# A new hand-written order for the start of an attention-plus-MLP kernel, with ten instead of twelve head pairs turned by TensorE and a changed end

## The chip, the cores and the metric

The kernel runs on one core of one Trainium2 chip. The metric is the device time of one execution in microseconds (us); the number quoted for a kernel is the median of several executions. One execution is also profiled; all rows shown below are from such an execution.

## The reference, cut to what matters

Eight batches of twelve heads, 448 tokens, 64 numbers per head. Soft-capped attention, and then a two-layer network over the 3584 tokens, whose activation is a maximum of two products:

```python
scores = scale * q @ k.T                    # per head, 448 x 448
scores = cap * tanh(scores / cap)           # cap = 30
attn = exp(scores - max); attn /= sum
x = (attn @ v)  ->  [3584, 768]
h1 = x @ w1; h2 = x @ w2                    # 768 -> 1024
out = maximum(h1, h2) @ w_out               # 1024 -> 768
```

## The kernel before, in words

**Algebra.** The maximum of h1 and h2 is written as relu(x @ (w1 - w2)) + x @ w2. So the kernel forms `wd_sb` = w1 - w2 (six blocks of 128 rows, one per 128 columns of x) and `wm_sb` = w2 @ w_out once, at the start, and then computes out = relu(x @ wd) @ w_out + x @ wm.

**Attention.** Two heads are a pair (48 pairs, numbered i), two pairs a quad (24 quads, numbered t). q and k have to lie with the head's 64 numbers along the partitions. For pairs below `NX` TensorE turns them (28 transposes of 64x64 per pair, with `ident` as the moving operand) and VectorE copies them to `qkT`; for later quads a transposing DMA on SP's queue does it. Tokens are taken seven per row (448 = 64 x 7), so six of a row's tokens make three full blocks of 128 keys and the seventh of both heads makes a "left" block.

**The order is written by hand.** `ORDER` is a text of steps, run through a table `STEPS`; each step issues its instructions to fixed engines, and every engine runs its own instructions strictly in the order in which the text put them. The place of a load in the text therefore only says what it stands behind on POOL's queue. The steps that are spoken of:

- On POOL's queue: `lk i`, `lq i` (load k or q of a pair, cast to bf16 by the DMA; for pairs from NX on, k is loaded in two parts and all runs are 64 numbers long), `lv t p` (v of a quad in four parts: two for `vp`, two for `vl`), `lw1 c`, `lw2 c` (a 128-row block of w1, w2), `lwo h` (half of w_out), and `sub c 1` (the subtraction that makes block c of `wd_sb`). `sub c 0` is the same on VectorE.
- On PE: `X i` (turn a pair), `W c` (turn a block of w2), `P c h n` (n of the eight matmuls, 128x384, that make a block of `wm_sb`), `S i j` (scores of one key block for the two heads of a pair), `L t` (scores of the left block of a quad), `Y t` (row sums), `V t u` (attn @ v), `M x y n` (n steps of two MLP groups at once, x on the upper and y on the lower 64 rows of the array; -1 is nobody).
- On ACT: `T i j`, `TL t` (tanh of one score tile), `E`, `EL` (exp). On DVE: `XC`, `WC`, `PC` (copies of what PE turned or premultiplied out of PSUM), `Y1` to `Y3` and `N` (normalize into `xT`), `A`, `B` (sums of exps), `ev g` (evacuate group g).
- On SP: `cr t` (the transposing DMA of a quad), `st b t` (store 128 rows of the result).

There are 120 MLP groups; `stage1` groups have 6 blocks of 128 rows and `stage2` groups 14. A group's 128-row block is done as two half matmuls of 64 rows, and two groups share the array, one on each half. Group 0 needs all six blocks of `wd_sb`. The last two groups, 118 and 119, are the two halves (384 columns each) of the last 128 rows of the result.

**Buffers that tie queues together.** `kqs` has two buffers, one for even and one for odd quads; a load of q or k for quad t waits until quad t-2 was turned. `vp`/`vl` have two buffers; a load of v for quad t waits for `V` of quad t-2. Score tiles have two PSUM buffers, shared by `S`, `L` and `V`. `qkT` has two buffers. The loads from POOL take eight semaphores in turn, so a load is issued only when the load eight places before it has landed.

Of the kernel before, what the change touches and what calls it, by code (L numbers as in the profile page):

```python
# [10 lines left out]
ld0 k; ld0 q; ms; lk 1 0; lq 1 0; lk 2 0; lw2 1; lwo 0; lq 2 0; cd k; lw2 0; cd q; X 0 0; lw2 2; lwo 1; lk 3 0;  # L11
X 1 1; XC 0; lq 3 0; lw1 0; XC 1; S 0 0; S 0 1; T 0 0; W 1 2; T 0 1; S 0 2; WC 1; L 0; T 0 2; lv 0 0; OP 1 0 3;
P 1 0 2; E 0 0 3; S 1 0; lv 0 1; X 2 0; P 1 0 1; XC 2; P 1 0 1; lv 0 2; W 0 1; P 1 0 2; WC 0; TL 0; P 1 0 2;
lv 0 3; W 2 2; PC 1 0; T 1 0; OP 0 0 0; P 0 0 1; WC 2; S 1 1; P 0 0 1; EL 0; P 0 0 1; S 1 2; P 0 0 2; T 1 1;
P 0 0 3; OP 2 0 1; P 2 0 2; PC 0 0; T 1 2; P 2 0 1; S 2 0; P 2 0 2; E 1 0 2; P 2 0 1; S 2 1; P 2 0 2; lw2 3;
OP 1 1 3; P 1 1 2; PC 2 0; P 1 1 2; lq 4 0; T 2 0; P 1 1 4; lq 5 0; E 1 2 3; X 3 2; PC 1 1; T 2 1; S 2 2; XC 3;
lk 4 0; OP 0 1 0; P 0 1 4; T 2 2; sub 0 1; P 0 1 4; OP 2 1 1; P 2 1 1; PC 0 1; L 1; Y 0 3; TL 1; lq 6 0; V 0 0;
Y1 0; E 2 0 3; lw2 4; V 0 1; Y2 0; lk 5 0; Y3 0; S 3 0; lq 7 0; N 0 0; W 3 2; lw1 3; P 2 1 1; N 0 1; T 3 0;
X 4 0; lw2 5; WC 3; lv 1 0; EL 1; S 3 1; XC 4; S 3 2; P 2 1 1; lv 1 1; P 2 1 1; T 3 1; P 2 1 1; W 4 3; lv 1 2;
P 2 1 1; T 3 2; lv 1 3; WC 4; X 5 2; lq 8 0; E 3 0 2; S 4 0; XC 5; S 4 1; lk 6 0; P 2 1 2; OP 4 1 0; P 4 1 1;  # L20
lk 7 0; sub 3 0; P 4 1 4; T 4 0; P 4 1 3; PC 2 1; OP 3 1 3; P 3 1 1; lq 9 0; E 3 2 3; W 5 2; PC 4 1; S 4 2;
WC 5; lw1 2; P 3 1 1; T 4 1; P 3 1 4; T 4 2; lk 8 0; P 3 1 2; OP 3 0 1; P 3 0 1; PC 3 1; lk 9 0; L 2; Y 1 0;
TL 2; lv 2 0; V 1 0; lv 2 1; Y1 1; E 4 0 3; lv 2 2; V 1 1; Y2 1; Y3 1; lv 2 3; S 5 0; lw1 1; N 1 0; X 6 2;
lv 3 0; N 1 1; T 5 0; X 7 3; sub 2 1; XC 6; EL 2; S 5 1; XC 7; S 5 2; X 8 0; T 5 1; X 9 2; XC 8; lv 3 1; T 5 2;
S 6 0; lv 3 2; XC 9; P 3 0 1; E 5 0 2; P 3 0 1; lv 3 3; S 6 1; P 3 0 1; lq 10 0; P 3 0 2; sub 1 0; P 3 0 2;
lk 10 0; OP 5 0 3; P 5 0 1; T 6 0; P 5 0 2; lk 11 0; P 5 0 2; PC 3 0; P 5 0 1; E 5 2 3; P 5 0 1; lq 11 0;
S 6 2; P 5 0 1; lw1 4; OP 4 0 0; P 4 0 1; T 6 1; P 4 0 1; PC 5 0; P 4 0 1; lw1 5; P 4 0 3; T 6 2; P 4 0 1;
lk 12 0; P 4 0 1; L 3; PC 4 0; lk 12 1; Y 2 2; TL 3; lq 12 0; V 2 0; Y1 2; E 6 0 3; lk 13 0; V 2 1; lk 13 1;
Y2 2; Y3 2; lq 13 0; S 7 0; N 2 0; X 10 1; sub 4 1; N 2 1; T 7 0; X 11 3; EL 3; S 7 1; S 7 2; OP 5 1 0;
P 5 1 1; A 3 0 1; P 5 1 1; T 7 1; P 5 1 2; XC 10; sub 5 1; P 5 1 3; T 7 2; P 5 1 1; XC 11; S 8 0; O 0 2;  # L30
M 0 -1 1; PC 5 1; M 0 -1 1; E 7 0 2; M 0 -1 1; S 8 1; M 0 -1 2; A 3 0 2; lv 4 0; M 0 -1 1; O 1 1; M 1 -1 2;
H 0; lv 4 1; M 1 -1 1; T 8 0; M 1 0 1; A 3 1 1; M 1 0 1; lv 4 2; M 1 0 1; O 2 3; M 2 0 1; B 3 0; E 7 2 3;
M 2 0 1; lv 4 3; S 8 2; M 2 0 1; H 1; B 3 1; M 2 1 1; lk 14 0; M 2 1 1; T 8 1; M 2 1 1; ev 0; O 3 0; M 3 1 1;
lk 14 1; M 3 1 2; T 8 2; H 2; A 3 1 2; M 3 2 1; lq 14 0; M 3 2 2; ev 1; O 4 2; M 4 2 1; lk 15 0; L 4; M 4 2 1;
lk 15 1; TL 4; Y 3 1; V 3 0; lq 15 0; Y1 3; E 8 0 3; V 3 1; Y2 3; Y3 3; S 9 0; M 4 2 1; lv 5 0; N 3 0; M 4 3 2;
N 3 1; M 4 3 1; lv 5 1; O 5 1; M 5 3 2; T 9 0; H 4; M 5 3 1; lv 5 2; ev 2; S 9 1; M 5 4 1; ev 3; lv 5 3;
M 5 4 1; EL 4; M 5 4 1; S 9 2; A 4 0 1; O 6 3; M 6 4 3; T 9 1; H 5; A 4 0 2; M 6 5 1; cr 6; M 6 5 2; ev 4;
O 7 0; M 7 5 1; T 9 2; M 7 5 1; S 10 0; H 6; M 7 5 1; M 7 6 1; E 9 0 2; M 7 6 1; ev 5; S 10 1; M 7 6 1; O 8 2;
M 8 6 2; H 7; M 8 6 1; M 8 7 2; ev 6; T 10 0; M 8 7 1; O 9 1; M 9 7 1; A 4 1 1; M 9 7 2; E 9 2 3; lk 16 0; H 8;
S 10 2; ev 7; M 9 8 3; lk 16 1; B 4 0; M 9 8 1; T 10 1; M 9 8 2; lq 16 0; B 4 1; M 9 8 2; T 10 2; M 9 8 2;  # L40
lk 17 0; A 4 1 2; M 9 8 1; O 10 3; M 10 8 2; lk 17 1; M 10 8 1; L 5; lq 17 0; Y 4 0; TL 5; V 4 0; Y1 4; V 4 1;
E 10 0 3; Y2 4; Y3 4; S 11 0; M 10 9 1; lv 6 0; N 4 0; M 10 9 2; M 8 9 1; N 4 1; lv 6 1; M 8 9 3; H 10;
M 8 9 1; lv 6 2; S 11 1; T 11 0; A 5 0 1; M 8 9 2; lv 6 3; M 8 9 1; O 11 0; M 11 9 1; A 5 0 2; EL 5; M 11 9 1;
S 11 2; M 11 9 1; ev 8; M 11 10 2; T 11 1; M 11 10 1; ev 9; M 11 10 1; cr 7; M 11 10 3; T 11 2; M 11 10 1;
S 12 0; M 11 10 1; st 0 0; M 11 10 2; E 11 0 2; O 12 2; M 12 10 1; S 12 1; H 11; M 12 10 2; M 12 11 2; H 10 2;
M 12 11 1; M 10 11 2; H 12; M 10 11 1; T 12 0; A 5 1 1; M 10 11 4; B 5 0; M 10 11 1; E 11 2 3; lk 18 0; O 13 1;
M 13 11 1; S 12 2; M 13 11 1; B 5 1; lk 18 1; M 13 11 1; M 13 12 1; T 12 1; M 13 12 1; ev 10; M 13 12 1;
lq 18 0; M 13 12 2; A 5 1 2; T 12 2; M 13 12 1; lk 19 0; M 13 12 2; ev 11; M 13 12 1; lk 19 1; L 6; Y 5 3;
TL 6; V 5 0; lq 19 0; Y1 5; st 0 1; V 5 1; E 12 0 3; Y2 5; Y3 5; S 13 0; M 13 12 1; lv 7 0; N 5 0; M 13 12 1;
O 14 0; M 14 12 2; H 13; lv 7 1; N 5 1; M 14 12 1; M 14 13 2; lv 7 2; H 12 2; S 13 1; T 13 0; A 6 0 1;  # L50
M 14 13 1; M 12 13 1; lv 7 3; M 12 13 2; H 14; A 6 0 2; EL 6; M 12 13 1; S 13 2; M 12 13 3; T 13 1; M 12 13 1;
O 15 3; M 15 13 1; cr 8; M 15 13 1; ev 12; M 15 13 1; M 15 14 1; T 13 2; M 15 14 1; ev 13; S 14 0; M 15 14 1;
O 16 2; M 16 14 1; E 13 0 2; M 16 14 1; H 15; S 14 1; M 16 14 1; st 0 2; M 16 15 2; ev 14; M 16 15 1; O 17 1;
M 17 15 2; H 16; T 14 0; M 17 15 1; A 6 1 1; M 17 16 3; ev 15; O 18 0; M 18 16 1; E 13 2 3; lk 20 0; S 14 2;
M 18 16 1; H 17; B 6 0; M 18 16 1; lk 20 1; M 18 17 1; T 14 1; M 18 17 1; ev 16; M 18 17 1; lq 20 0; O 19 3;
M 19 17 2; B 6 1; T 14 2; M 19 17 1; lk 21 0; H 18; ev 17; M 19 18 1; lk 21 1; M 19 18 2; A 6 1 2; O 20 2;
M 20 18 1; lq 21 0; M 20 18 2; L 7; ev 18; Y 6 1; TL 7; V 6 0; Y1 6; V 6 1; E 14 0 3; Y2 6; Y3 6; S 15 0;
M 20 19 1; lv 8 0; N 6 0; M 20 19 2; N 6 1; O 21 0; M 21 19 1; lv 8 1; M 21 19 2; H 20; lv 8 2; S 15 1; T 15 0;
# [12 lines left out]
M 28 27 2; H 26 2; A 8 1 2; M 28 27 1; lq 24 0; M 26 27 2; T 18 2; M 26 27 1; lk 25 0; M 26 27 1; L 9; lk 25 1;
Y 8 0; TL 9; V 8 0; Y1 8; lq 25 0; V 8 1; E 18 0 3; Y2 8; Y3 8; S 19 0; M 26 27 1; lv 10 0; N 8 0; M 26 27 3;
# [131 lines left out]
def kernel(  # L204
# [11 lines left out]
    nc = tc.nc  # L216
# [19 lines left out]
    NS = 3
    W2T = 4
    R7 = S // 64
# [178 lines left out]
    def turned_by_pe(t):  # L417
        return 2 * t < NX

# [267 lines left out]
```

## Time and profile before

| | us |
|---|---|
| median of 3 runs (lowest, highest) | 348.4 (348.33, 350.44) |
| the profiled execution | 348.68 |
| its span from first to last instruction | 346.9 |
| PE busy | 327.1 |
| ACT busy | 274.2 |
| DVE busy | 229.5 |
| POOL busy | 175.6 |
| mean granted TensorE clock | 0.99 |

The span is what the profile shows of the profiled execution; 1.78 us of its time lie outside it. Busy time is the union of an engine's instructions. Rows of the timeline give start, duration, engine, line of the code, what was written and read, and in square brackets how long the engine was idle before and what ended that.

### The profile page before, as it was taken

The page shows a single profiled execution, that of the slowest core. Times are in us where ns is not written, and L with a number is a line of the kernel's source. Part 1 is how long each engine was busy: PE and PEld are TensorE (multiplying, and loading weights), DVE is VectorE, ACT ScalarE, POOL GpSimd, SP SyncE. Part 2 cuts the span into 40 slices and gives each one's busy share as a digit, 9 for nine tenths or more (in the row PEclk, how much of TensorE's full clock was granted, in tenths as well). Part 3 has the DMA queues.
Part 4 walks back from the last instruction along what each step waited for, and adds up shares of the span by engine and source line. Part 5 has one row for each costly group of instructions (what it writes and reads, how often), then busy time and mean ns, then how long its engine had stood idle before and what let it go on. Part 6 is the DMA issues. An engine that isn't in the chain of part 4 may idle for free.

```text
span 346.9 us, 9713 instructions
## 1 busy us (share of the span) xinstructions
PE 327.1 (94%) x4100; PEld 197.6 (57%) x4100; DVE 229.5 (66%) x408; ACT 274.2 (79%) x265; POOL 175.6 (51%) x250
## 2 busy tenths in 40 slices
PE   3699997899999999999999999999999999999994
PEld 2355553355586656456656555555875555568762
DVE  3146767488678856886697668768876868774321
ACT  2768999299998999899989998999899989920000
POOL 8338798928437457195592859285658302000000
PEclk9999999699999999999999999999999999999999
DMA  8998999989999999999999999999999964031033
GB/s 128 202 225 158 206 187 192 81 112 86 149 155 112 147 174 107 162 135 99 164 199 118 101 194 215 119 104 170 174 133 109 166 124 79 1 92 49 2 93 91
DMA packets 130988, 46.09 MB, mean 133 GB/s; under 512 B 108288, under 2 KB 125952, under 8 KB 130944
## 3 DMA queue, kind: packets, MB, share of 16 engines
q0 software_dynamic: 93184, 25.74, 74.2%
q1 hardware_dynamic: 37616, 19.50, 28.6%
q8 instruction: 32, 0.52, 0.7%
q10 hardware_dynamic: 144, 0.23, 0.3%
q14 instruction: 12, 0.10, 0.1%
HBM read 48.76 MB, written 11.01 MB: 172 GB/s over the span
## 4 chain that ended last, share of the span: by engine, by line
PE 70%; DMA 12%; ACT 6%; issue 4%; POOL 4%; DVE 4%; SPq 0%; POOLq 0%; DVEq 0%
PE mm L563 52%; PE s L448 7%; PE s L531 5%; DMA osb<-in_moe_w_dram 4%; DMA gT<-in_moe_w_dram 4%; ACT e L469 4%; DMA xT<-in_moe_w_dram 3%; PE s L461 2%; PE s L535 2%; POOL kqs L306 2%; PE mm L506 2%; ACT e L453 1%; POOL wd_sb L356 1%; DVE osb L616 1%; DMA out_dram<-osb 1%
## 5 line engine op out<-in xcount | busy, mean ns | idle before, releaser
L453 ACT ACTIVATE e<-s 128x896 bf16<-128x896 f32 x144 | 127.8, 929 | 14.5 <-PE s L448 10.3
L469 ACT ACTIVATE e<-e 128x2688 bf16<-128x2688 bf16 (+2 forms) x72 | 122.9, 1709 | 0.0
L563 PE MATMUL mm<-wo_sb,gT 64*128 64x384 bf16 x896 | 120.3, 323 | 0.0
L563 PE MATMUL mm<-wm_sb,xT 64*128 64x384 bf16 x672 | 105.6, 323 | 0.0
L563 PE MATMUL mm<-xT,wd_sb 64*128 64x448 bf16 x768 | 101.5, 356 | 4.2 <-POOL wd_sb L356 3.2
L313 POOL DMA_DIRECT2D kqs<-in_k_dram x72 | 53.1, 741 | 77.3 <-DMA qkT<-kqs 77.3
L563 PEld LDWEIGHTS <-gT 64*128 64x128 bf16 x896 | 62.5, 94 | 25.4 <-issue 0.4
L563 PEld LDWEIGHTS <-wd_sb 64*128 64x128 bf16 x768 | 55.6, 95 | 26.0 <-issue 4.6
L563 PEld LDWEIGHTS <-xT 64*128 64x128 bf16 x672 | 52.9, 94 | 19.1 <-issue 1.0
L448 PE MATMUL s<-qkT 64*128 64x448 bf16 x288 | 56.9, 361 | 1.7 <-ACT e L453 1.5
L584 DVE TENSOR_SCALAR gT<-mm 128x448 bf16<-128x448 f32 x64 | 39.7, 621 | 14.5 <-PE mm L563 13.1
L616 DVE COPY osb<-mm 128x384 f32<-128x384 f32 x56 | 30.7, 555 | 27.5 <-PE mm L563 23.7
L481 DVE TENSOR_TENSOR esum<-e 128x896 bf16<-128x896 bf16 x42 | 26.1, 621 | 26.8 <-ACT e L469 15.1
L327 POOL DMA_DIRECT2D vp<-in_v_dram x48 | 30.4, 640 | 21.4 <-PE s L535 17.6
L531 PE MATMUL s<-e,vp 128*32 128x448 bf16 x576 | 35.8, 352 | 0.0
L313 POOL DMA_DIRECT2D kqs<-in_q_dram x36 | 34.8, 967 | 1.2 <-issue 1.1
L465 ACT ACTIVATE el<-s 128x896 bf16<-128x896 f32 x24 | 22.0, 916 | 16.2 <-PE s L461 15.8
L448 PEld LDWEIGHTS <-qkT 64*128 64x128 bf16 x288 | 17.6, 94 | 26.7 <-issue 15.3
L327 POOL DMA_DIRECT2D vl<-in_v_dram x48 | 29.3, 620 | 2.4 <-DMA gT<-in_moe_w_dram 2.4
L544 DVE TENSOR_TENSOR xT<-s,inv 128x448 bf16<-128x448 f32 x48 | 27.7, 620 | 2.6
L481 DVE TENSOR_TENSOR esum<-esum,e 128x896 bf16<-128x896 bf16 x42 | 27.5, 655 | 2.1 <-PE mm L563 0.4
L486 DVE TENSOR_TENSOR esum<-esum,el 64x896 bf16<-64x896 bf16 x42 | 25.9, 617 | 1.8 <-PE mm L563 1.0
(47 smaller groups left out, 235.2 us busy)
## 6 DMA issues: line engine op xcount, KB each, us to landing
out_dram<-osb SPq DMA_DIRECT2D x54, 192.0 KB, 4.2
vp<-in_v_dram POOLq DMA_DIRECT2D x48, 160.0 KB, 6.0
kqs<-in_q_dram POOLq DMA_DIRECT2D x47, 112.0 KB, 4.7
kqs<-in_k_dram POOLq DMA_DIRECT2D x72, 56.0 KB, 3.5
osb<-in_moe_w_dram POOLq DMA_DIRECT2D x4, 512.0 KB, 6.1
gT<-in_moe_w_dram POOLq DMA_DIRECT2D x6, 256.0 KB, 6.8
wo_sb<-in_moe_w_out_dram POOLq DMA_DIRECT2D x2, 768.0 KB, 12.4
kqs<-in_k_dram POOLq DMA_DIRECT2D x11, 112.0 KB, 4.7
```

What stands on the lines that cost most here:

```text
L313: nc.gpsimd.dma_start(out=to, in_=x)
L327: nc.gpsimd.dma_start(out=to, in_=x)
L448: nc.tensor.matmul(s[:, h, :S], k_of(t, o, h, j), q_of(t, o, h))
L453: nc.scalar.activation(expo[i][:, 2 * j : 2 * j + 2, :], slots[i, j][:, :, :S], AF.Tanh, scale=scale / cap)
L469: nc.scalar.activation(e, e, AF.Exp, scale=float(cap))
L481: nc.vector.tensor_add(d, e[:, 0:2, :] if j == 1 else d, e[:, 2 * j : 2 * j + 2, :])
L486: nc.vector.tensor_add(d, d, left_e[t][r, :, :])
L531: nc.tensor.matmul(ps[r, u, :S], vp[t % VB][:, m, 2 * j, u::2], expo[2 * t + o][:, 2 * j + h, :], start=(j == 0), stop=False)
L544: nc.vector.tensor_mul(x, vals[t][:, u, :S], sums[t, 3])
L563: ins = nc.tensor.matmul(self.ps, w[r], x[r], start=first, stop=self.at == [self.n, self.n]).ins
L584: nc.vector.tensor_relu(gT[b // 2][:, f, cs], ps)
L616: nc.vector.tensor_copy(o[:, hs], ps)
```

## The change

- `NX` goes from 12 to 10: pairs 10 and 11 (quad 5) are turned by the transposing DMA (`cr 5`), not by PE.
- For the five quads that PE turns, v is loaded with three tokens per row (two loads of 64 rows x 4 heads x 192 numbers instead of x 320 numbers); `transposes` places k's tokens to match, and `values` picks its block accordingly.
- `transposes` goes through the two 64x64 corners of the array in turn, not seven transposes in one and then seven in the other.
- `ORDER` is new up to the first steps of group 0. `S 0` no longer waits for other work of PE; the last block of w1 (`lw1 4`) stands on POOL's queue behind `lq 10`; four of the six subtractions are VectorE's instead of two. From `L 4` to group 116 the list of PE steps is the same, except for the PSUM banks; the list of ACT's steps is the same throughout, but for the copy at the very end. In POOL's list later on, v of a quad often stands between the k and q of two pairs instead of behind them.
- Groups 118 and 119 are done with whole 128-row matmuls, one after the other (`step(2)`).
- A store of 128 rows is one DMA instead of two. The last group is evacuated in two parts of 192 columns, by VectorE and ScalarE, and each part is stored from a queue of its own (SP, ACT).

The order, first up to group 0 and then at the end:

```diff
-ld0 k; ld0 q; ms; lk 1 0; lq 1 0; lk 2 0; lw2 1; lwo 0; lq 2 0; cd k; lw2 0; cd q; X 0 0; lw2 2; lwo 1; lk 3 0;
-X 1 1; XC 0; lq 3 0; lw1 0; XC 1; S 0 0; S 0 1; T 0 0; W 1 2; T 0 1; S 0 2; WC 1; L 0; T 0 2; lv 0 0; OP 1 0 3;
-P 1 0 2; E 0 0 3; S 1 0; lv 0 1; X 2 0; P 1 0 1; XC 2; P 1 0 1; lv 0 2; W 0 1; P 1 0 2; WC 0; TL 0; P 1 0 2;
-lv 0 3; W 2 2; PC 1 0; T 1 0; OP 0 0 0; P 0 0 1; WC 2; S 1 1; P 0 0 1; EL 0; P 0 0 1; S 1 2; P 0 0 2; T 1 1;
-P 0 0 3; OP 2 0 1; P 2 0 2; PC 0 0; T 1 2; P 2 0 1; S 2 0; P 2 0 2; E 1 0 2; P 2 0 1; S 2 1; P 2 0 2; lw2 3;
-OP 1 1 3; P 1 1 2; PC 2 0; P 1 1 2; lq 4 0; T 2 0; P 1 1 4; lq 5 0; E 1 2 3; X 3 2; PC 1 1; T 2 1; S 2 2; XC 3;
-lk 4 0; OP 0 1 0; P 0 1 4; T 2 2; sub 0 1; P 0 1 4; OP 2 1 1; P 2 1 1; PC 0 1; L 1; Y 0 3; TL 1; lq 6 0; V 0 0;
-Y1 0; E 2 0 3; lw2 4; V 0 1; Y2 0; lk 5 0; Y3 0; S 3 0; lq 7 0; N 0 0; W 3 2; lw1 3; P 2 1 1; N 0 1; T 3 0;
-X 4 0; lw2 5; WC 3; lv 1 0; EL 1; S 3 1; XC 4; S 3 2; P 2 1 1; lv 1 1; P 2 1 1; T 3 1; P 2 1 1; W 4 3; lv 1 2;
-P 2 1 1; T 3 2; lv 1 3; WC 4; X 5 2; lq 8 0; E 3 0 2; S 4 0; XC 5; S 4 1; lk 6 0; P 2 1 2; OP 4 1 0; P 4 1 1;
-lk 7 0; sub 3 0; P 4 1 4; T 4 0; P 4 1 3; PC 2 1; OP 3 1 3; P 3 1 1; lq 9 0; E 3 2 3; W 5 2; PC 4 1; S 4 2;
-WC 5; lw1 2; P 3 1 1; T 4 1; P 3 1 4; T 4 2; lk 8 0; P 3 1 2; OP 3 0 1; P 3 0 1; PC 3 1; lk 9 0; L 2; Y 1 0;
-TL 2; lv 2 0; V 1 0; lv 2 1; Y1 1; E 4 0 3; lv 2 2; V 1 1; Y2 1; Y3 1; lv 2 3; S 5 0; lw1 1; N 1 0; X 6 2;
-lv 3 0; N 1 1; T 5 0; X 7 3; sub 2 1; XC 6; EL 2; S 5 1; XC 7; S 5 2; X 8 0; T 5 1; X 9 2; XC 8; lv 3 1; T 5 2;
-S 6 0; lv 3 2; XC 9; P 3 0 1; E 5 0 2; P 3 0 1; lv 3 3; S 6 1; P 3 0 1; lq 10 0; P 3 0 2; sub 1 0; P 3 0 2;
-lk 10 0; OP 5 0 3; P 5 0 1; T 6 0; P 5 0 2; lk 11 0; P 5 0 2; PC 3 0; P 5 0 1; E 5 2 3; P 5 0 1; lq 11 0;
-S 6 2; P 5 0 1; lw1 4; OP 4 0 0; P 4 0 1; T 6 1; P 4 0 1; PC 5 0; P 4 0 1; lw1 5; P 4 0 3; T 6 2; P 4 0 1;
-lk 12 0; P 4 0 1; L 3; PC 4 0; lk 12 1; Y 2 2; TL 3; lq 12 0; V 2 0; Y1 2; E 6 0 3; lk 13 0; V 2 1; lk 13 1;
-Y2 2; Y3 2; lq 13 0; S 7 0; N 2 0; X 10 1; sub 4 1; N 2 1; T 7 0; X 11 3; EL 3; S 7 1; S 7 2; OP 5 1 0;
-P 5 1 1; A 3 0 1; P 5 1 1; T 7 1; P 5 1 2; XC 10; sub 5 1; P 5 1 3; T 7 2; P 5 1 1; XC 11; S 8 0; O 0 2;
-M 0 -1 1; PC 5 1; M 0 -1 1; E 7 0 2; M 0 -1 1; S 8 1; M 0 -1 2; A 3 0 2; lv 4 0; M 0 -1 1; O 1 1; M 1 -1 2;
...
+ld0 k; ld0 q; ms; lk 1 0; lwo 0; lk 2 0; lq 1 0; lw2 0; cd k; lk 3 0; cd q; lw2 2; X 0 0; lq 2 0; lq 3 0; XC 0;
+S 0 0; S 0 1; T 0 0; T 0 1; S 0 2; T 0 2; lw2 1; E 0 0 3; lwo 1; lk 4 0; X 1 1; XC 1; lv 0 0; W 0 2; lv 0 1;
+L 0; WC 0; S 1 0; TL 0; lv 0 2; OP 0 0 3; P 0 0 1; W 2 0; T 1 0; lv 0 3; EL 0; S 1 1; lw2 3; WC 2; S 1 2;
+X 2 1; T 1 1; X 3 2; XC 2; T 1 2; lv 1 0; W 1 0; XC 3; E 1 0 2; S 2 0; WC 1; S 2 1; P 0 0 7; T 2 0; OP 2 0 1;
+P 2 0 2; PC 0 0; P 2 0 3; E 1 2 3; P 2 0 1; S 2 2; P 2 0 2; T 2 1; PC 2 0; T 2 2; lv 1 1; OP 0 1 2; P 0 1 5;
+lv 1 2; P 0 1 3; OP 2 1 0; P 2 1 1; lv 1 3; P 2 1 1; PC 0 1; P 2 1 3; lw2 5; L 1; Y 0 3; TL 1; lq 4 0; V 0 0;
+lw2 4; Y1 0; E 2 0 3; V 0 1; Y2 0; lq 5 0; Y3 0; S 3 0; lk 5 0; N 0 0; W 3 1; P 2 1 1; N 0 1; lv 2 0; P 2 1 1;
+T 3 0; P 2 1 1; OP 1 0 2; P 1 0 1; WC 3; P 1 0 1; lv 2 1; S 3 1; EL 1; P 1 0 1; PC 2 1; lv 2 2; S 3 2; P 1 0 1;
+T 3 1; P 1 0 2; lv 2 3; P 1 0 2; OP 1 1 3; P 1 1 1; T 3 2; P 1 1 1; PC 1 0; P 1 1 1; lk 6 0; X 4 1; E 3 0 2;
+P 1 1 1; XC 4; P 1 1 4; lk 7 0; S 4 0; PC 1 1; S 4 1; T 4 0; W 4 0; lw1 5; W 5 2; WC 4; E 3 2 3; OP 3 0 1;
+P 3 0 1; lq 6 0; S 4 2; WC 5; X 5 3; T 4 1; lq 7 0; P 3 0 1; XC 5; P 3 0 1; lw1 2; P 3 0 1; T 4 2; P 3 0 2;
+lw1 0; L 2; Y 1 0; TL 2; lq 8 0; V 1 0; lq 9 0; Y1 1; E 4 0 3; V 1 1; lw1 3; Y2 1; Y3 1; S 5 0; N 1 0; P 3 0 1;
+lk 8 0; P 3 0 1; OP 4 1 2; P 4 1 1; N 1 1; P 4 1 2; T 5 0; P 4 1 1; lw1 1; PC 3 0; X 6 3; EL 2; sub 5 0;
+lk 9 0; S 5 1; S 5 2; X 7 0; T 5 1; XC 6; P 4 1 2; T 5 2; XC 7; P 4 1 1; lq 10 0; S 6 0; sub 2 0; P 4 1 1;
+OP 5 0 1; P 5 0 1; E 5 0 2; P 5 0 1; S 6 1; P 5 0 2; PC 4 1; P 5 0 1; lw1 4; P 5 0 3; T 6 0; sub 0 1; OP 4 0 3;
+P 4 0 2; PC 5 0; P 4 0 3; E 5 2 3; P 4 0 1; S 6 2; P 4 0 2; T 6 1; OP 3 1 0; P 3 1 2; PC 4 0; P 3 1 1; lv 3 0;
+P 3 1 2; T 6 2; P 3 1 2; sub 3 0; lv 3 1; L 3; Y 2 2; lv 3 2; TL 3; V 2 0; lv 3 3; Y1 2; E 6 0 3; V 2 1; Y2 2;
+lk 10 0; Y3 2; S 7 0; N 2 0; sub 1 1; X 8 1; N 2 1; X 9 3; T 7 0; XC 8; P 3 1 1; EL 3; S 7 1; XC 9; S 7 2;
+OP 5 1 2; P 5 1 1; lk 10 1; P 5 1 1; PC 3 1; P 5 1 1; T 7 1; P 5 1 1; A 3 0 1; P 5 1 2; lk 11 0; P 5 1 2;
+T 7 2; sub 4 0; O 0 1; M 0 -1 1; lk 11 1; S 8 0; M 0 -1 1; E 7 0 2; M 0 -1 1; S 8 1; PC 5 1; lq 11 0; M 0 -1 3;
...
-M 117 116 7; st 7 4; M 117 116 2; O 118 1; M 118 116 2; H 117; M 118 116 1; M 118 117 2; H 116 2; M 118 117 1;
-M 116 117 2; H 118; M 116 117 6; O 119 3; M 119 117 2; ev 116; M 119 117 1; M 119 118 2; ev 117; M 119 118 7;
-st 7 5; M 119 118 2; M -1 118 2; H 119; M -1 118 1; M -1 119 2; H 118 2; M -1 119 1; M 118 119 8; M -1 119 2;
-ev 118; M -1 119 1; ev 119; st 7 6;
+M 117 115 1; M 117 116 2; ev 115; M 117 116 7; st 7 4; M 117 116 2; M -1 116 2; H 117; M -1 116 1; M -1 117 2;
+H 116 2; M -1 117 1; M 116 117 8; M -1 117 2; ev 116; M -1 117 1; O 118 3; M 118 118 1; ev 117; M 118 118 7;
+st 7 5; M 118 118 6; O 119 0; M 119 119 2; ev 118; M 119 119 12; ev 119; st 7 6;
```

The functions:

```diff
-    NX = 12
+    NX = 10
...
     # load_v
         if part < 2:
             to = vp[t % VB].rearrange("p h j d -> p h (j d)")[r]
-            x = src[:, :, D * a : D * (a + 5)]
+            if turned_by_pe(t):
+                to = to[:, :, : NJ * D]
+                x = src[:, :, NJ * D * a : NJ * D * (a + 1)]
+            else:
+                x = src[:, :, D * a : D * (a + 5)]
...
     # transposes
-            for a in range(2):
-                r = slice(64 * a, 64 * a + 64)
-                for j in range(R7):
-                    to = c * S + j * D
+            for j in range(R7):
+                for a in range(2):
+                    r = slice(64 * a, 64 * a + 64)
+                    to = c * S + (j if c or j == R7 - 1 else 2 * (j % NJ) + j // NJ) * D
                     nc.tensor.transpose(ps[r, to : to + 64], x[r, c * S + j * D : c * S + (j + 1) * D], ident[r, r])
...
     # values
-                    ps[r, u, :S], vp[t % VB][:, m, 2 * j, u::2], expo[2 * t + o][:, 2 * j + h, :], start=(j == 0), stop=False
+                    ps[r, u, :S], vp[t % VB][:, m, j if turned_by_pe(t) else 2 * j, u::2], expo[2 * t + o][:, 2 * j + h, :], start=(j == 0), stop=False
...
     # Group.step
+            if h == 2:
+                w, x = self.unit(self.at[0])
+                self.at = [self.at[0] + 1] * 2
+                nc.tensor.matmul(self.ps, w, x, start=first, stop=self.at[0] == self.n)
+                return
...
     # store
-        for a in range(2):
-            nc.sync.dma_start(out=rows(b, j0 + a, 1)[0], in_=osb[64 * a : 64 * a + 64, :])
+        nc.sync.dma_start(out=rows(b, j0, 2), in_=osb)
...
     # stage2, done
-            nc.vector.tensor_copy(o[:, hs], ps)
-            if b == B - 1 and t == 6:
-                for a in range(2):
-                    to = out[b * S : (b + 1) * S, hs].rearrange("(r j) n -> j r n", j=R7)[R7 - 2 + a]
-                    nc.sync.dma_start(out=to, in_=o[64 * a : 64 * a + 64, hs])
+            if (b, t) != (B - 1, 6):
+                nc.vector.tensor_copy(o[:, hs], ps)
+                return
+            to = out[b * S : (b + 1) * S, :].rearrange("(r j) n -> j r n", j=R7)[R7 - 2 :]
+            mid = half * (DM // 2) + DM // (4 if half else 2)
+            c = slice(hs.start, mid)
+            nc.vector.tensor_copy(o[:, c], ps[:, : mid - hs.start])
+            nc.sync.dma_start(out=to[:, :, c], in_=o[:, c])
+            if half:
+                c = slice(mid, hs.stop)
+                nc.scalar.copy(o[:, c], ps[:, mid - hs.start :])
+                nc.scalar.dma_start(out=to[:, :, c], in_=o[:, c])
...
     # moe
         for _ in range(n):
+            if x == y:
+                groups[x].step(2)
+                continue
```

## The prediction

> **What bounds the kernel now.** I read the page first, for the engines' shares; then windows by stage; then PE's timeline, for a milestone that both kernels pass; then the chain of waits and POOL's timeline for the start; last the end.
>
> ```profile
> PE 327.1 (94%) x4100; PEld 197.6 (57%) x4100; DVE 229.5 (66%) x408; ACT 274.2 (79%) x265; POOL 175.6 (51%) x250
> ...
> 55.00:60.00 5.00, 3.72 (x23) 1.50 (x21) 4.11 (x5) 5.00 (x6) 3.27 (x3) 1.00 1.62 190
> 60.00:65.00 5.00, 3.03 (x16) 1.29 (x18) 1.33 (x3) 1.79 (x3) 5.00 (x6) 0.51 0.52 60
> 65.00:70.00 5.00, 5.00 (x52) 2.41 (x52) 2.83 (x5) 2.03 (x3) 4.17 (x6) 0.81 1.32 93
> ...
> 250.00:300.00 50.00, 49.57 (x635) 29.50 (x626) 37.71 (x68) 47.75 (x46) 18.06 (x27) 1.00 0.88 111
> 300.00:320.00 20.00, 19.07 (x233) 13.70 (x231) 12.43 (x22) 5.99 (x7) 0.00 (x0) 1.00 0.25 61
> 320.00:330.00 10.00, 10.00 (x121) 7.28 (x119) 3.62 (x6) 0.00 (x0) 0.00 (x0) 1.00 0.01 3
> ```
>
> The numbers behind the window's length are busy us of PE, weight loads, DVE, ACT, POOL, then the granted clock, the DMA share and GB/s. ACT is nearly as full as PE while attention lasts, but it ends near 306, and PE then works alone for 36 us. So PE's work and PE's idle time set the end, and time lost early is not regained. The one bad stretch is 55 to 70: PE idles, and the clock falls to 0.51 and 0.81.
>
> The milestone is `L t`, PE's left scores of a quad:
>
> ```profile
> 11.12 0.59 PE L461 MATMUL s<-qkT 64*64 64x448 bf16 x4
> 27.57 0.38 PE L461 MATMUL s<-qkT 64*64 64x448 bf16 x4
> 39.56 0.38 PE L461 MATMUL s<-qkT 64*64 64x448 bf16 x4
> 50.81 0.38 PE L461 MATMUL s<-qkT 64*64 64x448 bf16 x4
> 68.45 0.38 PE L461 MATMUL s<-qkT 64*64 64x448 bf16 x4
> 80.41 0.38 PE L461 MATMUL s<-qkT 64*64 64x448 bf16 x4
> ```
>
> L0 to L5. Two intervals stand out: L0 to L1 takes 16.45 us and L3 to L4 17.64, where the others take 11.25 to 12.0. The chain of waits and POOL's rows tell why:
>
> ```profile
> 3.19 6.43 DMA gT<-in_moe_w_dram
> 9.91 14.55 DMA osb<-in_moe_w_dram
> 50.58 9.15 DMA xT<-in_moe_w_dram
> 59.79 2.13 POOL wd_sb L356
> 61.97 2.79 PE mm L563 x12
> ```
>
> The last block of w1 is issued at 50.58 and lands at 59.73; POOL subtracts until 61.9; group 0 waits for it (idle 0.80 and 2.44 us).
>
> **The change, part by part.** From L4 to group 116 the steps of PE and ACT are the same list, so this stretch keeps its length: cost 0. What hides the rest there: a v load now stands ahead of the second pair's q and k in POOL's queue; these then land some 11 us after `L t`, and their transposing DMA is due 1.5 periods (18 us) after it. If that cover went, PE would wait at `S` by what is over, every period. The merged stores take 27 issues of about 0.6 us off SP, which waits anyway: 0. So the working is for L4, and for the end.
>
> Prices of PE work, start to start in dense stretches at full clock: P 0.174 (12 in 2.09, 46.86 to 48.95); S 0.29; X 0.62 a pair (56 transposes in 1.23, 42.56 to 43.79); L 0.31; Y with both V 2.28 (39.88 to 42.16); W 0.5; a slot of M 0.187 at 448 columns.
>
> (a) *Up to L1.* `T 0 0` needs one turned pair, not two: 0.45 us earlier, 7.3. `S 0 2` no longer stands behind `W 1`, so ACT's wait of 1.74 goes and exp of pair 0 ends at 12.2. But `X 1` needs `lq 1`, now behind the first half of w_out. Landings before: 5.7 for the first load; w_out's half takes 4.1 behind its predecessor (3.71+10.0 against 9.62); a q or k 0.6; and the first big load takes 1.4 more than later ones of its size. So X1 at 5.7+4.2+1.4+1.2 = 12.5. At the slow early speed (56 transposes 2.26, a W 0.95) X1, W0 (its block lands at 13.75) and L0 give L0 at 14.7, 3.6 *later* than before. Then the second pair has what it needs: `lq 2`, `lq 3`, `lw2 1` land by 18, where before PE stood 2.07 for w_out and ACT 3.0. ACT's list from 14.7 gives `T 2 0` near 21; PE is at `S 2 1` near 20.4. From there to L1 are 28 P and one S: 4.87+0.29, so L1 = 25.7, against 27.57: **-1.9**. Bounds: without the 1.4 X1 starts at 11.1 and the gain is 3.3; with the slow clock lasting to 24 it is 0.
>
> (b) *L1 to L2.* 25 P instead of 24: +0.17. (c) *L2 to L3.* 33 P for 23, +1.74; two X for four, -1.25; ACT was without idle here, so half the relief elsewhere counts: **+0.4** for b and c, before the transposes.
>
> (d) *L3 to L4.* Work before: L 0.31, Y and V 2.28, six S 1.74, two X 1.25, eight P 1.39, 25 M slots 4.7: 11.65; it took 17.64. So the waits of 3.24 cost 5.99 with the slow clock behind them. After: one P more, 11.8; L1 to L2 took 12.0 for 11.3 of such work, so 12.2 to 12.4. Does w1 come in time? `lw1 4` stands behind `lq 10`, which waits for `X 7`. By the prices X7 ends 5.9 before L3; `lq 10` issues in 0.97, so `lw1 4` goes out 4.9 before L3. Group 0 asks for block 4 at its fifth step, 7.2 after L3; the DVE subtraction takes 1.23. So 10.8 us for a load that took 6.9 and 9.15 at the same place before: just enough. `sub 1 1`, POOL's later one, ends 3 after L3, and is asked for at 6.3. **-5.3**.
>
> (e) *Transposes in turn.* No row has two 64x64 corners alternating. Upper bound: full overlap, as the two halves of M have (0.163 a pair of 384 columns): 0.31 a pair saved. Lower: 0. The nearest row is `L`, whose four matmuls go through all four corners and take 0.31 for 4x0.187: overlap by two. I take a third of the bound over the six pairs between L1 and L4: **-0.6**; ACT's pace, 11.25 a quad, takes the rest.
>
> The Trainium skill ("TensorE: Matmul & The Clock Gate", Part 1, "Wait — 56ns, not 53.3ns?") says that matmuls start no less than about 25 ns apart however small; the rows here have 1.23/56 = 22 ns, slightly below. By the page (e) would be 0 and the sum 0.6 higher.
>
> (f) *The end.*
>
> ```profile
> 341.28 1.20 DVE L616 COPY osb<-mm 128x384 f32<-128x384 f32 x2 [3.35 <-PE mm L563]
> 341.86 2.39 SPq L620 DMA_DIRECT2D out_dram<-osb  x4
> ```
>
> PE ends at 341.89; DVE copies the last half to 342.48; four stores, the last issued at 343.67, landing 2.2 later at 345.85. After: a DVE copy of 192 columns, 0.36 (line through 621 ns for 448 columns and 555 for 384), issue, 2.1 to land: 344.4. ACT's copy waits for DVE in the built program: 0.35 more (bounds 0.25 and 0.92, its 896 columns), landing 344.8: -1.05. 28 whole matmuls, as P, 0.174 for 0.1635 of a pair of halves: +0.3. **-0.75** (0 to -1.4).
>
> Sum: -1.9+0.4-5.3-0.6-0.75 = -8.15 on 348.68, the profiled execution's own time: 340.5. The median lies 0.28 below that; with rounding I say **340.5**.
>
> **The rivals.** *The wait stays, only moved* (20%): `lw1 4` can't go before X7, and loads with a full queue ahead have taken 14.55 us (row above). Then group 0 waits about 2 us, and at before's ratio (5.99 lost for 3.24) that is 3.7: 344.2. For it: X7 is late in the new order. Against: POOL has no subtraction before it now, so the queue is not held up; the loads ahead are fewer (v of quad 3 stands behind).
>
> *Quad 5's transposing DMA is late* (7%, **slower**). POOL issues in order: `lq 10` after X7 (43.6), `lw1 4`, `sub 0 1`, four v loads, `sub 1 1`, the k's, `lq 11`: about 12 us of POOL time, to 56; landing 59. `cr 5` then takes 4.0 (row at 145.24) to 11.2 (row at 134.24): 63 to 70. `S 10 0` is due 7.5 after L4, at 69. If either subtraction waits for its w1 block by more than 3 us and the transposition takes the long value, qkT lands beyond 73.7; PE waits 4.5, the clock falls, 8.3 are lost, and from there the kernel is slower: about 350. Against: it needs both.
>
> *The start gains nothing* (8%): L1 at 27.6 because X1 is late and the clock cold; with a short wait for w1 besides, 344 to 346. For it: L0 itself moves 3.6 later, and PE idles from 8.3 to 12.5.
>
> **How the numbers follow.** The forecast has 65%, its own range 338 to 343. 340.5 is its time. Upper end of the range: the second and third case, 345.5; lower: the full (a) and (e), 337. Of this kernel about 1% can be told from no change, that is 344.9 and 351.9. Faster: 0.65, 0.12 of the first rival, 0.03 of the third: 0.80. Slower 0.06; within 1% 0.14.
>
> **What would show it.** Left scores near 14.7, 25.6, 37.6, 49, 61, and 12 a quad after that; no slice with a granted clock below 0.9 after 20 us; POOL's and DVE's `wd_sb` done before group 0's steps; last landing about 2.9 behind PE's end; PE's list shorter by 56 transposes and 28 M. It is wrong if L4 stands later than 65, if the quads after L4 are longer than 12.1 on average, or if PE idles at the scores of pair 10.

## The result, and the profile after

| | before | after |
|---|---|---|
| median, lowest to highest (us) | 348.5, 348.33 to 350.44 | 422.55, 419.59 to 428.27 |
| the profiled execution | 348.68 | 425.03 |
| its span | 346.9 | 423.3 |

The ratio is 1.208, with a 95% interval of 1.198 to 1.218: the changed kernel is a fifth slower, where 340.5 us were forecast. A ratio leaves out some disturbed executions that the medians still hold.

The page of the changed kernel comes first: each engine's busy time, and the 40 slices of PE, of the granted clock and of the DMA share.

```profile
PE 335.8 (79%) x4016; PEld 195.9 (46%) x4016; DVE 228.3 (54%) x408; ACT 276.9 (65%) x266; POOL 174.2 (41%) x250
...
PE   2899999996989739995989990797859937999920
...
PEclk9999999999899968999899996599988986999985
...
DMA  8999999975999499959999997956999982011211
```

PE has 84 fewer instructions than before, but 8.7 us more busy time. From the tenth slice on there are holes in PE's row, and the clock falls in or behind the large ones. A slice is 10.6 us, so the first nine slices, 95 us, are as full as they should be.

The milestones say the same. These are PE's rows of the left scores `L t`, L0, L1 and L4 of the changed kernel:

```profile
14.13 0.59 PE L465 MATMUL s<-qkT 64*64 64x448 bf16 x4
24.81 0.38 PE L465 MATMUL s<-qkT 64*64 64x448 bf16 x4
59.48 0.38 PE L465 MATMUL s<-qkT 64*64 64x448 bf16 x4
```

The forecast had 14.7, 25.7 and 61 here, so the new front delivers what it should. Later the quads go wrong. ACT's tanh of the left tile, quads 6, 7 and 8:

```profile
83.58 0.92 ACT L469 ACTIVATE el<-s 128x896 bf16<-128x896 f32 x1 [0.36 <-PE s L465]
...
96.03 0.92 ACT L469 ACTIVATE el<-s 128x896 bf16<-128x896 f32 x1 [1.10 <-PE s L465]
...
113.77 0.92 ACT L469 ACTIVATE el<-s 128x896 bf16<-128x896 f32 x1 [1.03 <-PE s L465]
```

From 83.58 to 96.03 is 12.45 us, from there to 113.77 it is 17.74. The waits (who waited for whom: us in total, times, the longest) name a cause. PE's and ACT's first, then POOL's and SP's:

```profile
PE s L452 <- DMA qkT<-kqs: 52.6, 10, 13.1
...
ACT e L457 <- PE s L452: 64.3, 19, 11.7
...
POOL kqs L313 <- DMA qkT<-kqs: 48.4, 12, 11.7
...
SPq L419 <- DMA kqs<-in_q_dram: 162.4, 19, 18.6
```

PE stands ten times at the scores of a pair, for 52.6 us, because the transposing DMA on SP's queue has not delivered `qkT`. That DMA has itself waited for POOL's loads of q. It did so for 162.4 us in 19 times; SP's wait for them before was 12.2 us in 7. POOL's own wait for the transposing DMA is no sign of the trouble: it comes of the two buffers of `kqs`, and was longer before (77.3 us). So the question is why the loads of q and k are late. The DMA issues of 78 to 84 us (KB each, median us from issue to landing):

```profile
out_dram<-osb SPq DMA_DIRECT2D x2, 384.0 KB
kqs<-in_q_dram POOLq DMA_DIRECT2D x2, 112.0 KB, 14.6
kqs<-in_k_dram POOLq DMA_DIRECT2D x4, 56.0 KB, 16.5
```

SP's queue and POOL's, around the same two stores:

```profile
76.51 1.79 SPq L419 DMA_TRANSPOSE qkT<-kqs  x1
78.35 5.81 SPq L607 DMA_DIRECT2D out_dram<-osb  x2
101.27 1.57 SPq L419 DMA_TRANSPOSE qkT<-kqs  x1
```

```profile
91.07 0.62 POOL L331 DMA_DIRECT2D vp<-in_v_dram  x1 [3.98 <-issue]
94.57 0.62 POOL L331 DMA_DIRECT2D vl<-in_v_dram  x1 [2.88 <-PE mm L572]
101.29 0.59 POOL L331 DMA_DIRECT2D vl<-in_v_dram  x1 [6.11 <-DMA kqs<-in_q_dram]
```

The two merged stores go out at 78.35 and 83.65. A load of k that goes out beside them takes 16.5 us to land, where the median in the page of before was 3.5. POOL then stands idle between its loads (3.98, 2.88, 6.11 us). The view names other releasers for the first two of these gaps, but the loads eight places before landed at 90.03, 94.03 and 101.01 us, and each next load goes out 0.3 to 1.0 us behind that: here the eight semaphores hold POOL up. So the next transposing DMA, whose q landed at 101.01, goes out at 101.27, and the left scores of quad 8 are late. From there on it repeats. A piece of the chain of waits (start, us, what):

```profile
101.27 5.53 DMA qkT<-kqs
...
128.36 21.06 DMA kqs<-in_q_dram
...
149.53 5.67 DMA qkT<-kqs
```

The transposing DMA itself takes 5.5 to 5.7 us; what is long is the load of q ahead of it, 21.06 us.

The stretches (length, busy us of PE, weight loads, DVE, ACT, POOL, granted clock, DMA share, GB/s):

```profile
80.00:100.00 20.00, 19.97 (x252) 13.00 (x250) 17.16 (x31) 18.54 (x19) 6.06 (x9) 1.00 0.95 96
...
140.00:160.00 20.00, 10.15 (x99) 4.65 (x93) 6.76 (x12) 10.08 (x10) 7.29 (x10) 0.77 0.69 83
250.00:300.00 50.00, 32.45 (x362) 18.93 (x356) 23.12 (x41) 29.79 (x29) 15.96 (x23) 0.83 1.03 93
...
400.00:424.00 24.00, 4.86 (x30) 2.66 (x28) 1.63 (x4) 0.32 (x1) 0.00 (x0) 0.71 0.12 46
```

The last row is the key. After 400 us all DMAs in progress are stores, PE ends at 404.9 and from there on the kernel only waits for them, and the DMA share is 0.12. The share is a mean over 16 engines; 0.12 of 16 is two engines. A merged store runs on two of the sixteen. Its 128 rows are 64 packets of 3072 B on each of the two; a packet of the two stores above took 0.136 us on average, so one store keeps two engines occupied for about 64 x 0.136 = 8.7 us. That is an estimate from these two numbers, and it is near what the trace has: the 256 packets of the two stores issued at 78.35 and 83.65 lie between 81.6 and 100.5.

The trace also records each packet by itself, and these records show the two engines directly. In the changed kernel two packets of stores are in flight at a time for 176.9 us, and more than two for 8 us in all (mostly those of the stores that are two DMAs in every kernel). While both stores are outstanding it is still two: for 12.4 of the 14 us from 86 to 100. From 95.2 to 101.0 eight loads are outstanding and none lands, yet the DMA share from 95 to 101 is 0.20: most engines are idle. That the loads have parts on all engines, and that what is missing of them stands behind the stores on these two, is the reading that fits; the records do not name the engine.

The Trainium skill ("DMA: Bandwidth & Descriptors", section "Why a DMA increments its semaphore by 16 and not by 1", paragraph "How many engines (k)") states a rule that fits this: each access pattern's slowest dimension that is not 1 is looked at, and the largest number up to 16 that divides both is how many engines are used. The merged store writes `2 x 64 x 768` from `128 x 768`, which by the rule makes 2 engines; the store of before, `64 x 768` from `64 x 768`, makes 16. The share of 0.12 and the two packets in flight agree with it. That page also says that a DMA of such a queue takes the lowest-numbered engines; by that all merged stores would share the same two. The trace agrees as far as it goes: two stores outstanding together have two packets in flight and not four.

### The profile page after: what moved, and what is told of

The parts are those of the page before. It is cut to its first block, busy times and chain, and to the rows that moved or that the text cites. A ratio compares the mean times of both kernels' runs of the same rounds, so it can differ in the third digit from the quotient of the medians.

```text
span 423.3 us, 9500 instructions
## 1 busy us (share of the span) xinstructions
PE 335.8 (79%) x4016; PEld 195.9 (46%) x4016; DVE 228.3 (54%) x408; ACT 276.9 (65%) x266; POOL 174.2 (41%) x250
## 4 chain that ended last, share of the span: by engine, by line
PE 46%; DMA 39%; POOL 4%; ACT 2%; DVE 2%; issue 2%; POOLq 0%; SPq 0%; DVEq 0%; ACTq 0%
PE mm L572 29%; DMA qkT<-kqs 21%; DMA kqs<-in_q_dram 5%; PE s L452 5%; DMA wo_sb<-in_moe_w_out_dram 5%; DMA vp<-in_v_dram 5%; DMA vl<-in_v_dram 4%; PE mm L386 3%; PE s L535 3%; POOL kqs L313 2%; ACT e L473 2%; PE s L465 1%; PE s L539 1%; PE mm L567 1%; PE mm L411 1%
## 5 line engine op out<-in xcount | busy, mean ns | idle before, releaser
L572 PE MATMUL mm<-wm_sb,xT 64*128 64x384 bf16 x648 | 108.3, 338 | 0.0
L572 PE MATMUL mm<-xT,wd_sb 64*128 64x448 bf16 x768 | 103.3, 361 | 1.0 <-DVE gT L593 0.8
L452 PE MATMUL s<-qkT 64*128 64x448 bf16 x288 | 57.8, 380 | 55.6 <-DMA qkT<-kqs 52.6
L313 POOL DMA_DIRECT2D kqs<-in_k_dram x76 | 55.8, 737 | 73.7 <-DMA qkT<-kqs 48.4
L572 PEld LDWEIGHTS <-wd_sb 64*128 64x128 bf16 x768 | 56.7, 97 | 22.9 <-issue 5.5
L452 PEld LDWEIGHTS <-qkT 64*128 64x128 bf16 x288 | 16.5, 97 | 83.6 <-DMA qkT<-kqs 56.7
L625 DVE COPY osb<-mm 128x384 f32<-128x384 f32 x54 | 29.6, 555 | 34.8 <-PE mm L572 33.9
L313 POOL DMA_DIRECT2D kqs<-in_q_dram x38 | 36.9, 971 | 9.6 <-DMA kqs<-in_k_dram 3.5
L485 DVE TENSOR_TENSOR esum<-esum,e 128x896 bf16<-128x896 bf16 x42 | 26.2, 624 | 1.8
```

What stands on the lines that cost most here:

```text
L313: nc.gpsimd.dma_start(out=to, in_=x)
L452: nc.tensor.matmul(s[:, h, :S], k_of(t, o, h, j), q_of(t, o, h))
L485: nc.vector.tensor_add(d, e[:, 0:2, :] if j == 1 else d, e[:, 2 * j : 2 * j + 2, :])
L572: ins = nc.tensor.matmul(self.ps, w[r], x[r], start=first, stop=self.at == [self.n, self.n]).ins
L625: nc.vector.tensor_copy(o[:, hs], ps)
```

## The experiments

Every kernel ran beside the kernel before on the same chip; the time before is given where it matters.

**The merged store undone, all else kept.**

```diff
 # store
-        nc.sync.dma_start(out=rows(b, j0, 2), in_=osb)
+        for a in range(2):
+            nc.sync.dma_start(out=rows(b, j0 + a, 1)[0], in_=osb[64 * a : 64 * a + 64, :])
 # done: the two stores of the last group likewise, each cut in two by a
-                nc.scalar.dma_start(out=to[:, :, c], in_=o[:, c])
+                for a in range(2):
+                    nc.scalar.dma_start(out=to[a, :, c], in_=o[64 * a : 64 * a + 64, c])
```

> The changed kernel with one thing undone: every store of 128 rows is again two DMAs of 64 rows (the last parts too, on the queues they have now). Theory T, that the merged store runs on few DMA engines and so holds up the loads that share them: L4 stays at 59.5, every quad after it takes 12.0, no wait of the scores for the transposing DMA above 1 us, 339 us (337 to 341). Rival R, that the new order of POOL's loads (v between the k and q of two pairs) and the extra transposing DMA make q and k late: the waits stay, 400 us or more.

Measured: 340.39 us (338.42 to 344.63), ratio 0.982 (0.975 to 0.989). The page, the left scores of quad 4, and the DMA issues of 78 to 84 us, as above:

```profile
PE 319.8 (95%) x4016; PEld 193.6 (58%) x4016; DVE 228.3 (68%) x408; ACT 274.5 (82%) x266; POOL 174.4 (52%) x250
...
PEclk9999999999999999999999999999999999999999
...
58.59 0.38 PE L465 MATMUL s<-qkT 64*64 64x448 bf16 x4
...
out_dram<-osb SPq DMA_DIRECT2D x3, 192.0 KB, 4.7
kqs<-in_k_dram POOLq DMA_DIRECT2D x5, 56.0 KB, 5.1
kqs<-in_q_dram POOLq DMA_DIRECT2D x2, 112.0 KB, 5.3
```

The clock is full in every slice, and k lands in 5.1 us where it took 16.5. The whole loss of the change is in the merged stores. SP's wait for loads of q is 46.0 us in 14 times here, against 162.4. The difference of the two profiled spans, 423.3 - 336.7 = 86.6 us, can be laid out by rows of the two kernels: PE's wait for the transposing DMA, 52.6 against 0.2, is 52.4; PE's busy time, 335.8 against 319.8 for the same 4016 instructions, is 16.0 that go with the lower clock (0.92 on the mean against 1.00); from PE's end to the end of the span, 18.4 against 4.8, is 13.6; PE's waits for v (2.7 and 1.3) are 4.0, and at the start 0.6 more for one load of q, which lies ahead of the first store and is not its doing. Together 86.6.

**The merged store alone, in the kernel before.** The same edit backwards, and nothing else of the change: new order, turned v and new end are all absent.

```diff
-        for a in range(2):
-            nc.sync.dma_start(out=rows(b, j0 + a, 1)[0], in_=osb[64 * a : 64 * a + 64, :])
+        nc.sync.dma_start(out=rows(b, j0, 2), in_=osb)
```

> The kernel before with the merged store alone (one DMA whose target is 2 x 64 x 768; the four stores of the very end as before). Theory T: the loads behind a store land in steps of about 4 us instead of 0.4 to 0.8, scores wait for the transposing DMA, 400 to 430 us. Rival R: 347 to 350, as before, since the order of loads is the old one.

Measured: 424.24 us (420.62 to 427.87). One edit in one place makes the old kernel as slow as the changed one. Its waits, and its clock:

```profile
PE s L531 <- DMA vp<-in_v_dram: 38.8, 8, 8.3
...
PEclk9999998999989968899698999599689995999996
```

The time is the expected one, the wait is not: here PE stands for v rather than for q and k (its wait for `qkT` is 3.4 us). In the old order v of a quad is issued behind k and q, and that would be why v suffers from the late landings; no run tries it by itself. The price is nearly the same. This also disposes of the rival that the new order of the loads was the cause.

**Is it the one DMA instead of two, or the shape?** Two DMAs per store again, but cut by columns, so that the target keeps the slowest dimension of 2 (`2 x 64 x 384`).

```diff
-        nc.sync.dma_start(out=rows(b, j0, 2), in_=osb)
+        for h in range(2):
+            c = slice(h * (DM // 2), (h + 1) * (DM // 2))
+            nc.sync.dma_start(out=rows(b, j0, 2)[:, :, c], in_=osb[:, c])
```

> The changed kernel with two DMAs a store, as many as before and as large as before (192 KB each), but cut by columns, so that each target is 2 x 64 x 384. Theory T (what counts is the slowest dimension of 2, which puts the DMA on two engines): as the changed kernel, 410 to 440 us. Rival S, that one large DMA of 384 KB, or fewer DMAs on SP, is what hurts: 339 to 345 us.

Measured: 439.32 us (435.28 to 443.36). PE's wait for the transposing DMA rose:

```profile
PE s L452 <- DMA qkT<-kqs: 68.6, 11, 14.4
```

So two DMAs of 192 KB don't help, and the size of one DMA is not the cause. Again two packets of stores are in flight at a time. That it is worse than the one DMA fits the packets: there are twice as many of half the length, and one takes 0.074 us on average, so a store keeps its two engines for 128 x 0.074 = 9.5 us and not 8.7. That is an estimate, and the reason is not tested further.

**Doses.** If the number of engines is the cause, other numbers must give other times. In the kernel with two DMAs per store, each 64-row store is cut once more, at row 63, 57 or 62:

```diff
-            nc.sync.dma_start(out=rows(b, j0 + a, 1)[0], in_=osb[64 * a : 64 * a + 64, :])
+            for p in (slice(0, 57), slice(57, 64)):
+                nc.sync.dma_start(out=rows(b, j0 + a, 1)[0][p], in_=osb[64 * a + p.start : 64 * a + p.stop, :])
```

> The kernel with two-DMA stores, where each 64-row store is cut into 63 rows and 1 row. If a DMA runs on the largest number of engines up to 16 that divides its rows, 63 rows run on 9 engines, 7 rows of 3 KB each: 7 x 0.136 = 1.0 us of an engine per store instead of 0.55 with 16. Theory T: 340 to 344 us. Rival S (a target with the shape 2 x 64 is slow by itself, whatever the engines): 339 to 342, as the two-DMA stores.

> As before it, cut into 57 rows (3 engines, 19 rows each, 2.6 us) and 7 rows (7 engines). Theory T: between, 345 to 390 us, with some waits of the scores for the transposing DMA. Rival S: 339 to 343.

> As before it, cut into 62 rows (2 engines, 31 rows each, 4.2 us, two such a store) and 2 rows (2 engines). The same two engines and the same bytes on each as with the merged store, but no target of shape 2 x 64. Theory T: 400 to 440 us. Rival S: 339 to 343.

Measured, with the ratio to the kernel before and PE's wait for the transposing DMA from each profile. The engines are by the rule of the Trainium skill's page named above; the rows per engine are worked out from them (both parts of both halves on the busiest engine, for one 128-row store), if the smaller part shares an engine with the larger:

| store of 64 rows as | engines of the larger part | rows per engine | median, us | ratio (95%) | PE's wait, us |
|---|---|---|---|---|---|
| 64 | 16 | 8 | 340.39 | 0.982 (0.975 to 0.989) | 0.2 |
| 63 + 1 | 9 | 16 | 341.74 | 0.978 (0.968 to 0.988) | 0.4 |
| 57 + 7 | 3 | 40 | 358.56 | 1.026 (1.018 to 1.033) | 11.6 |
| 62 + 2 | 2 | 64 | 418.27 | 1.197 (1.189 to 1.204) | 40.8 |
| 128 in one DMA, `2 x 64` (after) | 2 | 64 | 422.55 | 1.208 (1.198 to 1.218) | 52.6 |

The packet records bear the engines out. Of packets of stores there are two in flight at a time for 176.7 us with 62 + 2, three for 84.9 us with 57 + 7, nine for 14.8 us with 63 + 1, and with 64 rows up to sixteen, for 9.2 us. Each of these is the number that its kernel holds longest (with 64 rows, next to one packet alone).

The first row ran on another chip, where the kernel before took 347.95; for the three cuts it took 349.94. Nothing but the number of rows in a part distinguishes the three cuts: the bytes, the packets of 3072 B and the number of stores are the same. 62 + 2 with the old, plain 2-dimensional target has nearly the same loss as the merged store (its PE also waits 12.4 us for loads of q and v), and 63 + 1 has none that can be seen. So it is neither the 3-dimensional target nor the number of DMAs; what decides is on how many engines the rows lie. The step is steep between 3 engines and 2. The edit reaches 23 of the kernel's stores of 128 rows (four others, `t == 3`, are two DMAs in every kernel, and the last has its own code). By the packet's 0.136 us these 23 keep the busiest engine for 23 x 64 x 0.136 = 200 us at 64 rows per engine, 125 at 40, 50 at 16 and 25 at 8. That is an estimate; the loads' own packets come on top.

**The transposes in sevens again.** The kernel with two DMAs per store, with the two loops of `transposes` in the old order, seven in one 64x64 corner and then seven in the other.

```diff
-            for j in range(R7):
-                for a in range(2):
-                    r = slice(64 * a, 64 * a + 64)
+            for a in range(2):
+                r = slice(64 * a, 64 * a + 64)
+                for j in range(R7):
```

> The kernel with two-DMA stores, and with the transposes again seven in one corner of the array and then seven in the other. By the changed kernel's trace a pair costs 0.505 us when the corners take turns (56 in 1.01), by the one before 0.615. If PE sets the pace of the start, L4 comes 0.3 to 0.7 us later than with the corners in turn, and so does the end; if ACT sets it (11.25 us a quad), 0 to 0.2 later.

Measured: 341.27 us (340.43 to 345.45), ratio 0.983 (0.977 to 0.989), against 340.39 with the corners in turn: the medians differ by 0.9, which lies within the spread of either. In the profiles `L 4` moves from 58.59 to 60.21, 1.6 us, but that is no measure of the edit: the changed kernel, the one cut by columns and the three doses have the same start, all of it ahead of the first store, and their `L 4` lies between 58.81 and 60.13. From `L 1` to `L 4` five of these six kernels take 34.67 us, one 35.61, and the one in sevens 35.20. The price of a pair is clear from the trace. In the changed kernel, where 56 transposes follow one another:

```profile
50.78 1.07 PE L411 MATMUL mm<-ident,kqs 64*64 64x64 bf16 x56
51.79 0.34 PE L386 MATMUL mm<-wo_sb,w2T 128*128 128x384 bf16 x1
```

From 50.78 to 51.79 is 1.01 us for 56, 18 ns from start to start and 0.505 a pair, where seven in a row had 22 ns and 0.62. So alternating corners are worth 0.11 us a pair, 0.66 for six pairs, which the 0.53 from `L 1` to `L 4` would fit; in the total this is too small to be told from no difference.

**The old load of v.** The same kernel with five tokens per row for all quads.

```diff
-            if turned_by_pe(t):
-                to = to[:, :, : NJ * D]
-                x = src[:, :, NJ * D * a : NJ * D * (a + 1)]
-            else:
-                x = src[:, :, D * a : D * (a + 5)]
+            x = src[:, :, D * a : D * (a + 5)]
 # transposes
-                    to = c * S + (j if c or j == R7 - 1 else 2 * (j % NJ) + j // NJ) * D
+                    to = c * S + j * D
 # values
-vp[t % VB][:, m, j if turned_by_pe(t) else 2 * j, u::2]
+vp[t % VB][:, m, 2 * j, u::2]
```

> The kernel with two-DMA stores, with v of the first five quads loaded as in the kernel before (five tokens a row, 160 KB a load instead of 96), and k's tokens placed accordingly. The load queue then carries some 0.3 us more for each of these loads. If the queue sets the pace of the start, group 0 comes 1 to 2 us later and the end with it (341 to 343); if PE and ACT do, 0 to 0.5 later.

Measured: 340.0 us (339.06 to 344.47), ratio 0.970 (0.964 to 0.976), against 340.39 and 0.982 (0.975 to 0.989) for the load of three tokens. The ratios come from two chips whose times for the kernel before differ by 2 us, so they can't be set against each other to the last digit. A gain from the smaller load of v isn't seen in the times. In the profile `L 1` to `L 4` takes 35.69 us against 34.67, one execution against one, where the same start has also taken 35.61.

No run here has the new end apart from the rest; what is said of it below is read from the traces. Of all kernels run, those with two DMAs per store are the fastest (340.0, 340.4 and 341.3).

## Why the prediction was wrong, and where it was right

**The step that failed.** "The merged stores take 27 issues of about 0.6 us off SP, which waits anyway: 0." This priced a store by the time of its queue: one issue fewer. (The count was off as well: 23 stores are merged before the last one, since those with `t == 3` stay two DMAs.) It did not price the transfer. The step counted DMAs and bytes, and both were harmless; what changed was the outermost dimension of the target, from 64 to 2, and with it the number of engines from 16 to 2. In the place of the 0 stand 82 us by the medians (422.55 against 340.39) and 86 by the profiled executions. The diff showed it (`rows(b, j0, 2)` is `2 x 64 x 768`), and the profile of before had in its stores the row to compare with: 192 KB landed in 4.2 us at the median on sixteen engines. With 64 rows of a 128-row store on an engine in place of 8, the forecast should have had a term for what is late next. The sentences in front of it had the cover: q and k land some 11 us after `L t`, and are due at 18. That leaves 7 us, and a load that lands in 15 to 21 us and not in 4 to 5 uses up more. "If that cover went, PE would wait at `S` by what is over" is what happened, in ten periods.

**No rival had it.** The forecast's slower case, quad 5's transposing DMA late where PE's own turning ends, fell: with two DMAs per store, all else the same, PE waits for `qkT` once in the whole kernel, by 0.2 us. The mechanism of that rival, a late transposing DMA, a PE that stands and then a lower clock, did come about, but everywhere behind quad 6 and for another reason. The range, 337.0 to 345.5, rested on landings that the kernel before had shown (up to 14.55 us), and on no transfer that takes engines away from others.

**What the rest was worth.** With the stores in two DMAs the kernel is as forecast: 340.39 against 340.5, though its four executions lie 6 us apart, so the agreement to a tenth is luck. The terms, in the profiled execution of that kernel:

- (a) `L 0` 13.69 for 14.7, `L 1` 23.92 for 25.7: -3.65 where -1.9 was forecast, just beyond the upper bound of 3.3; in the five other kernels with this start it is -2.3 to -3.4. The term "the first big load takes 1.4 more" was too high: the half of w_out lands 4.5 behind its predecessor (5.66 to 10.12), where 4.2 + 1.4 were forecast. X1 does its half for k from 8.30 and its half for q from 11.31, where all of it was to start at 12.5. Of the 1.8 by which `L 1` is early, 1.0 is there at `L 0`; where the other 0.8 comes from is open.
- (b, c) `L 1` to `L 3` 22.98 us for 23.24 before: -0.26. Forecast were +0.4, and -0.4 of (e) for four of the six pairs, together 0.
- (d) `L 3` to `L 4` 11.69 for 17.64: -5.95. Forecast were -5.3 and -0.2 of (e). In the changed kernel `lw1 4` goes out at 43.81, group 0 starts at 54.04, and VectorE's subtraction of that block runs from 53.94 to 55.16; PE's weight load waits for it once, 0.3 us. "Just enough" was a fair reading, and the rival that put 2 us of waiting here fell.
- (e) -0.11 a pair, -0.66 for six: the third of the bound that the forecast took. The 18 ns between starts are below the floor of about 25 ns that the Trainium skill states ("TensorE: Matmul & The Clock Gate", Part 1, "Wait — 56ns, not 53.3ns?"), as the 22 ns of before were. By that page this term would have been 0.
- From `L 4` on, apart from the stores: ACT's quads take 11.99 us each, 12.0 before. Cost 0 holds.
- (f) The end of that kernel:

```profile
331.89 0.36 DVE L631 COPY osb<-mm 128x192 f32<-128x192 f32 x1 [1.72 <-PE mm L567]
...
332.33 0.32 ACT L636 COPY osb<-mm 128x192 f32<-128x192 f32 x1 [36.47 <-DMA out_dram<-osb]
...
332.68 1.20 ACTq L638 DMA_DIRECT2D out_dram<-osb  x2
```

VectorE's copy takes the forecast 0.36, ScalarE's 0.32 for 0.35, and it does start behind VectorE's. The last store is issued at 333.28 and lands at 335.27, 3.4 us behind PE's end, where the kernel before had 4.0 and the forecast 2.9: the second DMA of the half, which the forecast had merged away, takes its issue again. The whole matmuls start 0.164 apart (14 in 2.29), as two halves do, so the +0.3 for them was not paid. In the changed kernel, with merged stores, the span ends 18.4 us behind PE's end, against 4.8 here.

In sum the kernel with two DMAs gained 9.9 by `L 4` in its profiled execution where 7.4 was forecast (8.3 to 9.9 in the six kernels with this start), and 0.4 behind it where 0.75 was forecast; its profiled execution, 338.42, is the fastest of the four.

## What to carry to other kernels

A store is priced by how many engines its outermost dimension gives it, not by the number of its issues: before two DMAs are merged into one with an outer dimension of 2, write down both shapes, and ask how many rows each engine then has. A transfer that nobody waits for is not free when it takes the engines from transfers that somebody does wait for: look for the cover of those (here the loads of q, k and v, with eight outstanding and two buffers), and ask what follows when a landing takes longer than the cover. In a profile the sign is a stretch in which only that transfer runs: a DMA share of 0.12 is two engines of sixteen.

## What the runs showed of the hardware that was not expected

- The price of few engines is not proportional. 9 engines in place of 16 cost nothing that can be measured, 3 cost 4 to 5% of the time (ratio 1.026 against 0.982), and 2 cost 22 to 23% (1.197 against 0.982; 418.27 against 340.39).
- A few transfers slowed all others: with 23 merged stores in the whole kernel, the median landing of k rose from 3.6 to 7.2 us on the page, and beside two of them from 5.1 to 16.5 us.
- Transposes of 64x64 that alternate between two corners of TensorE start every 18 ns, 22 in one corner.
